# Four column groups for sums and gate logits, and one transposition for the one-hots of q and k, in a routed attention with a mixture of experts behind it

## The chip, the cores and the metric

The kernel runs on one core of a Trainium2 chip. The metric is the device time of one execution in microseconds (us). The core has a matrix engine (PE; its weight loads are listed apart as PEld), a vector engine (DVE), a scalar engine (ACT), a general engine (POOL) and DMA queues. Each engine works through its own instructions in order and waits for others by semaphores. All data is computed on in SBUF and PSUM, memories of 128 partitions.

## What is computed

Attention in which a query sees only those keys that fall to the same of 16 centroids, for 4 batches of 8 heads, 768 rows of 64 numbers; then a mixture of 8 experts that gives each row to one expert:

```python
q_assign = argmax(q_n @ c_n.T)            # per head; rows and centroids normalized
k_assign = argmax(k_n @ c_n.T)
mask = q_assign[:, :, :, None] == k_assign[:, :, None, :]
scores = where(mask, q @ k.T / sqrt(D), -1e9)
attn = exp(scores - max(scores)); attn = attn / (sum(attn) + 1e-9)
x = (attn @ v) -> rows of H*D             # 3072 x 512
logits = x @ w_gate; e = argmax(logits); gate = softmax(logits)[e]
out = gate * (relu(x @ w1[e]) @ w2[e])
```

## The kernel before

Attention goes over 16 pairs of heads (4 batches, 4 pairs each). A pair has 12 units: two halves of the queries (384 each) by six blocks of 128 keys. Three units make a turn, so a pair takes four turns. In one turn PE computes the scores of three units, does the jobs that the schedule puts there, multiplies the exponentials of the turn before with v, and does more jobs.

The mask is part of the score. Each row of q and k has a one-hot vector of its centroid. A second matmul adds q's one-hots times (one-hots of k - 1) * 2^60, so a score whose centroids differ becomes hugely negative before the exponential:

```python
def score(u):
    ...
    for a in range(2):          # the two heads: partitions 0-63 and 64-127
        r = slice(a * D, (a + 1) * D)
        nc.tensor.matmul(ps[:, a, 0:HS], lhsT=qk[g][r, 1, ks], rhs=qk[g][r, 0, qs], start=True, stop=False)   # L673
    for a in range(2):
        r = slice(a * D, (a + 1) * D)
        nc.tensor.matmul(ps[:, a, 0:HS], lhsT=ohT[g][r, 1, ks], rhs=ohT[g][r, 0, qs], start=False, stop=True) # L676
    A[u] = ap.tile([P, 2, HS], F32, name="A")
    nc.scalar.activation(A[u], ps[:, :, 0:HS], AF.Exp)                                                        # L678
    ...   # DVE adds A[u] to T, the running sum over key blocks                                              # L681, L685
```

The one-hots are made two turns ahead. `similar` (L613) multiplies q and k with the centroids, into four column groups of 32 PSUM partitions (q or k, by half); ACT copies the result, three transposes (L624) bring rows back to the partitions; `assign` and `assign2` find the largest and write the one-hots. One turn ahead `put` transposes them:

```python
ohs = consts.tile([P, 2 * NQ, 2, D], BF16, name="oh")     # 12 blocks: q and k apart, 2 heads x 64 columns, 16 used

def assign2(g):
    ...
    nc.vector.tensor_tensor(ohs[:, :, :, 0:C], rank..., top..., op=ALU.is_equal)                               # L641

def put(g):
    ohT[g] = ohp.tile([P, 2, S], BF16, name="ohT")
    ps = ps_s.tile([P, 2, 512], F32, name="sps").bitcast(BF16)
    for w in range(2):
        for j in range(NQ):
            nc.tensor.transpose(ps[:, w, j * P : (j + 1) * P], ohs[...], ident_b)                             # L651
    nc.scalar.copy(ohT[g][:, 0, :], ps[:, 0, 0:S])                                                            # L655
    nc.vector.tensor_scalar(ohT[g][:, 1, :], ps[:, 1, 0:S], scalar1=BIG, scalar2=-BIG, op0=ALU.mult, op1=ALU.add)  # L656
```

When a pair is done, its sums (over the 128 partitions of T) and its share of the gate logits are computed two turns later, the logits from the not yet divided rows XT. Before, a half of the queries has one column group of 32 PSUM partitions: 16 columns of logits for both heads, and the two sums:

```python
def weigh(g):
    ps = ps_m.tile([P, 512], F32, name="mps")
    t = [T.pop((g, half)) for half in range(2)]
    for i in range(3):
        for half in range(2):
            nc.tensor.matmul(
                ps[half * 32 : (half + 1) * 32, 0:HS],
                lhsT=one_row[:, i, :] if i < 2 else wg[:, g % HP, :],
                rhs=t[half][:, i, :] if i < 2 else XT[g][:, half * HS : (half + 1) * HS],
                start=(i == 0), stop=(i == 2))                                                                # L711
    lsT[g] = stat.tile([64, HS], F32, name="lsT", bufs=1)
    nc.scalar.copy(lsT[g], ps[0:64, 0:HS])                                                                    # L718

def weigh2(g):
    ...
    for i in range(NQ // 2):
        nc.tensor.transpose(ps[:, i * 64 : (i + 1) * 64], lt[:, i * P : (i + 1) * P], ident[0:64, 0:64])      # L725
    ls = stat.tile([P, NQ, 32], F32, name="ls")
    nc.vector.tensor_copy(ls, ps[:, 0 : NQ * 32]...)                                                          # L727
    ...   # reciprocal of the sums (L730), logits times it (L734), added to lg (L741, L744)
```

`x_turn` (L754, L757) transposes XT back and divides it, `gate` (L766 to L775) computes the softmax of a batch's logits, `turn` (L599 to L606) transposes the next q and k. Where they share a turn, the order in each engine is that of the program: the DVE operations of `weigh2`, then three additions to T, then, after a batch's last pair, `gate`, then L656 of `put`, then L757.

After attention the experts' matmuls follow (L301, L345); while the last pair's sums are computed, the first layer of an early group of rows runs in between.

Of the kernel before, what the change touches and what calls it, by code (L numbers as in the profile page):

```python
# [8 lines left out]
F32 = mybir.dt.float32  # L9
BF16 = mybir.dt.bfloat16  # L10
# [3 lines left out]
ALU = mybir.AluOpType  # L14
# [5 lines left out]
BIG = float(2**60)  # L20
# [163 lines left out]
def kernel(  # L184
# [11 lines left out]
    nc = tc.nc  # L196
    B, H, S, D = q.shape
    C = centroids.shape[1]
    P = 128
    NQ = S // P  # L200
    HP = H // 2
    NG = B * HP
    HS = S // 2
# [3 lines left out]
    E = moe_w_gate.shape[1]  # L207
    F = moe_w1.shape[2]
    DB = Dm // P
# [14 lines left out]
    consts = ctx.enter_context(tc.tile_pool(name="consts", bufs=1))  # L224
# [5 lines left out]
    def fetch(e, i):  # L230
        i %= 3
        w1 = wpools[i].tile([P, DB, F], F32, name=f"w1_{i}")
        w2 = wpools[i].tile([P, FB, Dm], F32, name=f"w2_{i}")
        nc.sync.dma_start(out=w1, in_=moe_w1[bass.ds(e, 1)].rearrange("e (a p) f -> p (e a) f", p=P))
        nc.sync.dma_start(out=w2, in_=moe_w2[bass.ds(e, 1)].rearrange("e (a p) d -> p (e a) d", p=P))
        return w1, w2
# [3 lines left out]
    ident = consts.tile([P, P], F32)  # L240
    ident_b = consts.tile([P, P], BF16)
# [18 lines left out]
    ps_s = late.enter_context(tc.tile_pool(name="ps_s", bufs=NB, space=PSUM))  # L260
# [4 lines left out]
    def wide():  # L265
        return ps_s.tile([P, 2, 512], F32, name="sps")
# [236 lines left out]
    with ExitStack() as actx:  # L503
        ld = actx.enter_context(tc.tile_pool(name="ld", bufs=2))
        qkp = actx.enter_context(tc.tile_pool(name="qkp", bufs=2))
        ohp = actx.enter_context(tc.tile_pool(name="ohp", bufs=2))
        asg = actx.enter_context(tc.tile_pool(name="asg", bufs=2))
        ap = actx.enter_context(tc.tile_pool(name="ap", bufs=2 * NB))
        tp_ = actx.enter_context(tc.tile_pool(name="tsum", bufs=2))
        stat = actx.enter_context(tc.tile_pool(name="stat", bufs=2))  # L510
# [27 lines left out]
        wg_in = consts.tile([P, DB, E], F32)  # L538
# [6 lines left out]
        first_c = iota("first_c", [P, C], [[-1, C]], C, 0)  # L545
        first_e = iota("first_e", [P, E], [[-1, E]], E, 0)

        wg = consts.tile([P, DB, 32], F32)
        nc.gpsimd.memset(wg, 0.0)
        one_row = consts.tile([P, 2, 32], F32)  # L550
        nc.gpsimd.memset(one_row, 0.0)
        for a in range(2):
            r = slice(a * D, (a + 1) * D)
            nc.gpsimd.tensor_copy(wg[r, :, a * E : (a + 1) * E], wg_in[r])
            nc.gpsimd.memset(one_row[:, a, 2 * E + a : 2 * E + a + 1], 1.0)

        ohs = consts.tile([P, 2 * NQ, 2, D], BF16, name="oh")
        nc.gpsimd.memset(ohs, 0.0)


        csq = consts.tile([P, D], F32)
# [27 lines left out]
        qk, sims, ohT = {}, {}, {}  # L589
# [47 lines left out]
        def assign2(g):  # L637
            rank = sims.pop(g)
            top = asg.tile([P, G], F32, name="top")
            nc.vector.tensor_reduce(top, rank, axis=AX, op=ALU.max)  # L640
            nc.vector.tensor_tensor(  # L641
                ohs[:, :, :, 0:C], rank.rearrange("p (t a) c -> p t a c", a=2),
                top.rearrange("p (t a) -> p t a", a=2).unsqueeze(3).to_broadcast([P, 2 * NQ, 2, C]), op=ALU.is_equal,
            )

        def put(g):
            ohT[g] = ohp.tile([P, 2, S], BF16, name="ohT")
            ps = ps_s.tile([P, 2, 512], F32, name="sps").bitcast(BF16)
            for w in range(2):
                for j in range(NQ):  # L650
                    nc.tensor.transpose(  # L651
                        ps[:, w, j * P : (j + 1) * P],
                        ohs[:, (j % (NQ // 2)) * 4 + w * 2 + j // (NQ // 2)].rearrange("p a c -> p (a c)"), ident_b,
                    )
            nc.scalar.copy(ohT[g][:, 0, :], ps[:, 0, 0:S])  # L655
            nc.vector.tensor_scalar(ohT[g][:, 1, :], ps[:, 1, 0:S], scalar1=BIG, scalar2=-BIG, op0=ALU.mult, op1=ALU.add)  # L656


        A, T, O = {}, {}, {}
        X, XT = {}, {}  # L660
# [43 lines left out]
        lsT, rds = {}, {}  # L704

        def weigh(g):
            ps = ps_m.tile([P, 512], F32, name="mps")
            t = [T.pop((g, half)) for half in range(2)]
            for i in range(3):
                for half in range(2):  # L710
                    nc.tensor.matmul(  # L711
                        ps[half * 32 : (half + 1) * 32, 0:HS],
                        lhsT=one_row[:, i, :] if i < 2 else wg[:, g % HP, :],
                        rhs=t[half][:, i, :] if i < 2 else XT[g][:, half * HS : (half + 1) * HS],
                        start=(i == 0), stop=(i == 2),
                    )
            lsT[g] = stat.tile([64, HS], F32, name="lsT", bufs=1)
            nc.scalar.copy(lsT[g], ps[0:64, 0:HS])  # L718

        def weigh2(g):  # L720
            b, hp = divmod(g, HP)
            lt = lsT.pop(g)
            ps = ps_m.tile([P, 512], F32, name="mps")
            for i in range(NQ // 2):
                nc.tensor.transpose(ps[:, i * 64 : (i + 1) * 64], lt[:, i * P : (i + 1) * P], ident[0:64, 0:64])  # L725
            ls = stat.tile([P, NQ, 32], F32, name="ls")
            nc.vector.tensor_copy(ls, ps[:, 0 : NQ * 32].rearrange("p (t r) -> p t r", r=32))  # L727
            den = ls[:, :, 2 * E : 2 * E + 2]
            rds[g] = stat.tile([P, NQ, 2], F32, name="rd")
            nc.vector.reciprocal(rds[g], den)  # L730
            nc.gpsimd.tensor_copy(dens[:, g, :].rearrange("p (t a) -> p t a", a=2), den)

            lgh = stat.tile([P, NQ, 2, E], F32, name="lgh")
            nc.vector.tensor_tensor(  # L734
                lgh, ls[:, :, 0 : 2 * E].rearrange("p t (a e) -> p t a e", a=2),
                rds[g].unsqueeze(3).to_broadcast([P, NQ, 2, E]), op=ALU.mult,
            )
            lgb = lg.rearrange("p (b h i) e -> p b i h e", b=B, h=2)[:, b]
            lgv = lgh.rearrange("p (i h) a e -> p i h a e", h=2)
            if hp == 0:  # L740
                nc.vector.tensor_tensor(lgb, lgv[:, :, :, 0, :], lgv[:, :, :, 1, :], op=ALU.add)  # L741
            else:
                for a in range(2):
                    nc.vector.tensor_tensor(lgb, lgb, lgv[:, :, :, a, :], op=ALU.add)  # L744
# [50 lines left out]
        for g in range(NG):  # L795
            n = g * TG
            if g == 1:

                for f, a in ((turn, (g, 0)), (turn, (g, 1)), (similar, (g,)), (similar2, (g,))):
                    at(-1 if f is similar2 else -2, 1, f, *a)  # L800
            else:
                at(n - 4, 0, turn, g, 0)
                at(n - 4, 1, turn, g, 1)
                at(n - 3, 0, similar, g)
                at(n - 3, 1, similar2, g)
            at(n - 2, 0, assign, g)
            at(n - 2, 0, assign2, g)
            at(n - 1, 0, put, g)
            at(n + TH, 1, finish, g, 0)
            at(n + 2 * TH, 1, finish, g, 1)  # L810
            if g < NG - 1:
                at(n + TG + 2, 0, weigh, g)
                at(n + TG + 2, 1, weigh2, g)
                at(n + TG + 3, 1, x_turn, g, 0)
                at(n + TG + 4, 0, x_turn, g, 1)
                if g % HP == HP - 1:
                    at(n + TG + 3, 0, gate, g // HP)
                    at(n + TG + 4, 0, keep_rows, g // HP)
# [51 lines left out]
        n = NG * TG  # L870
        at(n + 1, 0, first_half, 0, 0, FB // 4)
        at(n + 1, 0, weigh, NG - 1)
        at(n + 1, 0, first_half, 0, FB // 4, FB // 2)
        at(n + 1, 0, weigh2, NG - 1)
        at(n + 1, 0, x_turn, NG - 1, 0)
        at(n + 1, 1, x_turn, NG - 1, 1)
# [28 lines left out]
    with tc.tile_pool(name="sm", bufs=1) as sm:  # L905
# [31 lines left out]
        for t0 in range(0, NT, TQ):  # L937
# [11 lines left out]
            op=ALU.is_le,  # L949
# [3 lines left out]
        den = dens.rearrange("p g t -> p (g t)")  # L953
# [60 lines left out]
    with tc.If(nx > XU):  # L1014
        with tc.For_i(XU, nx, 1) as i:
# [4 lines left out]
            g = dict(n=[P], rows=N, w=fetch(ex, 0), gi=lambda j: gi[:, 0:1], si=lambda j: gi[:, 1:2], apart=False)  # L1020
# [36 lines left out]
```

## Time and profile before

| what | value |
| --- | --- |
| time, median of 3 executions | 864.28 us (863.96 to 864.37) |
| span of the profiled execution | 862.4 us |
| first 430 us (attention) | PE busy 396.3 of the 400 us from 30 to 430, DVE 244.2, ACT 207.2, POOL 27.5 |
| rest (430 to 862.4 us) | PE busy 417.4 of 432.4 us, DVE 52.7, ACT 50.2 |
| L711, sums and logits | 128 + 64 instructions on PE |
| L651, transposes of one-hots | 192 on PE |
| L725, transposes of sums and logits | 48 on PE |
| L656, one-hots of k to SBUF | 16 on DVE, 551 ns each |

How to read it: an fp32 matmul of the program is two instructions on PE in the trace, except the transposes. The ends of matmuls are modelled and overlap, so the cost of a stretch on PE is best taken from start to start. A line of the timeline merges neighbours of one kind: start, time from the first start to the last end, engine, line, operation, output and inputs, shapes, count, and in brackets how long the engine had been idle before and what ended it.

### The profile page before, as it was taken

To read this page: it belongs to the slowest core of one execution; us is meant where nothing else is said; L and a number is where in the kernel's file an instruction comes from. 1 tells how busy PE (TensorE), PEld (TensorE's weight loads), DVE (VectorE), ACT (ScalarE), POOL (GpSimd) and SP (SyncE) were. 2 spreads that over 40 slices of the span, in tenths; PEclk is the share of its full clock that TensorE was granted. 3 is DMA by queue.
4 is the path that set the end of the run, shared out by engine and by line. 5 is a ranking of instruction groups with operands and counts; after the bars stand their busy time and mean duration, and the time that the engine had idled before them with its cause. 6 is when DMAs were issued, how large, how long until landed. Compare 5 with 4: busy or idle time off the path is not lost.

```text
span 862.4 us, 10765 instructions
## 1 busy us (share of the span) xinstructions
PE 832.5 (97%) x4397; PEld 435.3 (50%) x4397; DVE 307.7 (36%) x543; ACT 271.2 (31%) x422; POOL 107.4 (12%) x165
## 2 busy tenths in 40 slices
PE   4999999999999999999999999999999999999994
PEld 3444544444445444444576646645444454545472
DVE  2655566565565665875543101010101010101000
ACT  3554544554545555544311111111111111110010
POOL 3000000000000000130004211302020303010010
PEclk8999999999999999999999999999999999999998
DMA  9025320482222122210060245434242423312010
GB/s 203 1 57 217 88 55 11 121 251 56 55 81 59 46 55 56 93 38 1 8 274 15 66 141 205 159 110 152 110 150 110 164 98 119 136 67 90 24 38 7
DMA packets 76186, 81.69 MB, mean 95 GB/s; under 512 B 52831, under 2 KB 56927, under 8 KB 75616
## 3 DMA queue, kind: packets, MB, share of 16 engines
q1 hardware_dynamic: 70208, 60.82, 23.0%
q0 software_dynamic: 5248, 20.04, 6.5%
q8 instruction: 37, 0.61, 0.3%
q14 instruction: 21, 0.17, 0.1%
q10 hardware_dynamic: 672, 0.05, 0.1%
HBM read 68.26 MB, written 13.68 MB: 95 GB/s over the span
## 4 chain that ended last, share of the span: by engine, by line
PE 46%; issue 38%; POOL 8%; DVE 5%; ACT 1%; DMA 0%; POOLq 0%; ACTq 0%; DVEq 0%
PE sps L673 14%; PE O L693 14%; PE mps L711 4%; PE sps L676 3%; POOL out_dram L316 3%; POOL xg L270 3%; PE sps L599 3%; PE sps L301 2%; PE mps L613 2%; DVE T L685 2%; PE sps L754 2%; PE sps L651 1%; POOL oh_c L468 1%; PE mps L624 1%; PE sps L345 1%
## 5 line engine op out<-in xcount | busy, mean ns | idle before, releaser
L678 ACT ACTIVATE A<-sps 128x768 f32<-128x768 f32 x192 | 154.4, 810 | 71.1 <-PE sps L676 70.0
L301 PE MATMUL sps<-xgT,w 128*128 128x416 f32 (+2 forms) x640 | 175.2, 434 | 1.1 <-ACT xgT L290 1.1
L673 PE MATMUL sps<-qk 64*128 64x384 f32 x768 | 163.7, 501 | 0.5 <-DVE x L757 0.5
L345 PE MATMUL sps<-w,h_sb 128*128 128x512 f32 x368 | 160.6, 595 | 1.3 <-DVE h_sb L309 0.9
L301 PEld LDWEIGHTS sps<-xgT,w 128*128 128x128 f32 x640 | 111.1, 190 | 67.5 <-issue 49.8
L685 DVE TENSOR_TENSOR T<-T,A 128x768 f32<-128x768 f32 x128 | 122.6, 958 | 47.6 <-ACT A L678 37.6
L693 PE MATMUL O<-A,v_in 128*64 128x384 f32 x768 | 138.0, 494 | 0.0
L309 DVE TENSOR_SCALAR h_sb<-sps 128x416 f32<-128x416 f32 (+2 forms) x34 | 18.7, 550 | 316.6 <-PE sps L301 316.6
L345 PEld LDWEIGHTS sps<-w,h_sb 128*128 128x128 f32 x368 | 69.1, 190 | 91.7 <-issue 85.6
L673 PEld LDWEIGHTS sps<-qk 64*128 64x128 f32 x768 | 68.1, 187 | 36.5 <-issue 33.7
L693 PEld LDWEIGHTS O<-A,v_in 128*64 128x64 f32 x768 | 49.4, 136 | 69.7 <-issue 68.2
L315 ACT ACTIVATE zo<-sps,xg 128x512 f32<-128x512 f32 (+1 forms) x34 | 23.3, 685 | 180.0 <-PE sps L345 171.0
L316 POOL DMA_INDIRECT out_dram<-zo,s_idx x34 | 33.0, 970 | 319.0 <-ACT zo L315 316.1
L676 PE MATMUL sps<-ohT 64*128 64x384 bf16 x384 | 66.2, 324 | 2.2 <-DVE ohT L656 2.2
L311 ACT ACTIVATE h_sb<-sps 128x416 f32<-128x416 f32 (+2 forms) x34 | 16.5, 484 | 162.8 <-DVE h_sb L309 162.8
L681 DVE SCALAR_TENSOR_TENSOR T<-A 128x768 f32<-128x768 f32 x32 | 30.7, 959 | 82.1 <-ACT A L678 82.1
L634 POOL TENSOR_TENSOR sim<-sim,first_c 128x384 f32<-128x384 f32 x16 | 16.0, 997 | 291.3 <-DVE sim L633 291.3
L270 POOL DMA_INDIRECT xg<-x_rows,g_idx x34 | 33.3, 980 | 22.8 <-issue 9.8
L676 PEld LDWEIGHTS <-ohT 64*128 64x128 bf16 x384 | 22.1, 94 | 26.5 <-DVE ohT L656 5.4
L701 ACT COPY xT<-O 128x384 f32<-128x384 f32 x32 | 15.4, 481 | 31.4 <-PE O L693 31.4
L711 PE MATMUL mps<-T,one_row 128*32 128x384 f32 x128 | 23.7, 492 | 0.0
L345 PE MATMUL sps<-w,h 128*128 128x512 f32 x48 | 21.3, 597 | 1.4 <-ACT h L311 1.4
(191 smaller groups left out, 532.2 us busy)
## 6 DMA issues: line engine op xcount, KB each, us to landing
w<-in_moe_w_dram SPq DMA_DIRECT2D x20, 2048.0 KB, 8.7
x_rows<-x POOLq DMA_DIRECT2D x4, 1548.0 KB, 7.2
q_in<-in_q_dram SPq DMA_DIRECT2D x32, 192.0 KB, 4.5
k_in<-in_k_dram SPq DMA_DIRECT2D x32, 192.0 KB, 4.6
v_in<-in_v_dram SPq DMA_DIRECT2D x16, 384.0 KB, 3.4
xg<-x_rows,g_idx POOLq DMA_INDIRECT x34, 5.1
out_dram<-zo,s_idx POOLq DMA_INDIRECT x34, 2.9
csb<-in_centroids_dram ACTq DMA_DIRECT2D x1, 32.0 KB, 1.8
```

The lines of the kernel that those rows point to most:

```text
L270: nc.gpsimd.indirect_dma_start(out=g["xg"][0:m, j, :], out_offset=None, in_=x_d[0 : g["rows"], :], in_offset=bass.IndirectOffsetOnAxis(ap= ...
L301: nc.tensor.matmul(o, lhsT=g["w"][0][:, c, fb * P : (fb + 1) * P], rhs=g["xT"][:, c, :cols], start=(c == 0), stop=(c == DB - 1),)
L316: ins = nc.gpsimd.indirect_dma_start(out=out[:, :], out_offset=bass.IndirectOffsetOnAxis(ap=g["si"](j)[0:m], axis=0), in_=zo[0:m], in_offs ...
L345: nc.tensor.matmul(zp, lhsT=g["h"][:, fb, j * P : (j + 1) * P], rhs=g["w"][1][:, fb, :], start=(fb == 0), stop=(fb == FB - 1),)
L599: nc.tensor.transpose(ps[:, i * P : (i + 1) * P], rows[g, "qk"[w]][:, j].rearrange("p a d -> p (a d)"), ident)
L673: nc.tensor.matmul(ps[:, a, 0:HS], lhsT=qk[g][r, 1, ks], rhs=qk[g][r, 0, qs], start=True, stop=False)
L676: nc.tensor.matmul(ps[:, a, 0:HS], lhsT=ohT[g][r, 1, ks], rhs=ohT[g][r, 0, qs], start=False, stop=True)
L678: nc.scalar.activation(A[u], ps[:, :, 0:HS], AF.Exp)
L681: nc.vector.scalar_tensor_tensor(T[g, half], in0=A[u - 1], scalar=1e-9 / P, in1=A[u], op0=ALU.add, op1=ALU.add)
L685: nc.vector.tensor_tensor(T[g, half], T[g, half], A[u], op=ALU.add)
L693: nc.tensor.matmul(O[g, half][a * D : (a + 1) * D, 0:HS], lhsT=rows[g, "v"][:, a, j, :], rhs=a_[:, a, :], start=(j == 0), stop=(j == NQ - 1),)
L711: nc.tensor.matmul(ps[half * 32 : (half + 1) * 32, 0:HS], lhsT=one_row[:, i, :] if i < 2 else wg[:, g % HP, :], rhs=t[half][:, i, :] if i ...
```

## The change

`weigh` uses all four column groups of 32 partitions, one per half and head, so each has to take only two matmuls, the sum and the logits of its own head, where a group took three before. Its result then fills 128 partitions, and the three transposes in `weigh2` are 128x128. In `put` the one-hots of q and k of a block of rows lie side by side (32 columns each, head by head) and are transposed together: six transposes and not twelve. A transposed block holds q's one-hots of a head at partitions 0 (or 64) and k's at 32 (or 96). ACT copies the whole block as the q side; for the k side, which must lie at the same partitions as q's, DVE reads k's 16 rows of each head and writes them shifted by 32 partitions into a tile whose other rows stay zero from the start. So what ACT copied of k is multiplied by zero. The two tiles for that are kept for the whole kernel and used in turn, as the pool's two buffers were before.

```diff
-        wg = consts.tile([P, DB, 32], F32)
+        wg = consts.tile([P, DB, 2, 32], F32)
-        one_row = consts.tile([P, 2, 32], F32)
+        one_row = consts.tile([P, 32], F32)
+        nc.gpsimd.memset(one_row[:, E : E + 1], 1.0)
...
-        ohs = consts.tile([P, 2 * NQ, 2, D], BF16, name="oh")
+        ohs = consts.tile([P, NQ, 2, 2, 32], BF16, name="oh")
         nc.gpsimd.memset(ohs, 0.0)
+        ohTs = []
+        for i in range(2):
+            t = consts.tile([P, 2, S], BF16, name=f"ohT{i}")
+            nc.gpsimd.memset(t[:, 1, :], 0.0)
+            ohTs.append(t)
...
         def assign2(g):
-            nc.vector.tensor_tensor(
-                ohs[:, :, :, 0:C], rank.rearrange("p (t a) c -> p t a c", a=2), ..., op=ALU.is_equal,
-            )
+            for w in range(2):
+                nc.vector.tensor_tensor(
+                    ohs.rearrange("p (i h) a w c -> p i (h a) w c", h=2)[:, :, :, w, 0:C], v(rank, w), ...,
+                    op=ALU.is_equal,
+                )
...
         def put(g):
-            ohT[g] = ohp.tile([P, 2, S], BF16, name="ohT")
-            ps = ps_s.tile([P, 2, 512], F32, name="sps").bitcast(BF16)
-            for w in range(2):
-                for j in range(NQ):
-                    nc.tensor.transpose(ps[:, w, j * P : (j + 1) * P], ohs[...], ident_b)
-            nc.scalar.copy(ohT[g][:, 0, :], ps[:, 0, 0:S])
-            nc.vector.tensor_scalar(ohT[g][:, 1, :], ps[:, 1, 0:S], scalar1=BIG, scalar2=-BIG, op0=ALU.mult, op1=ALU.add)
+            oh = ohT[g] = ohTs[g % 2]
+            ps = wide()[:, 0, :].bitcast(BF16)
+            for j in range(NQ):
+                nc.tensor.transpose(ps[:, j * P : (j + 1) * P], ohs[...], ident_b)
+            nc.scalar.copy(oh[:, 0, :], ps[:, 0:S])
+            for a in range(2):
+                nc.vector.tensor_scalar(
+                    oh[a * D : a * D + C, 1, :], ps[a * D + 32 : a * D + 32 + C, 0:S],
+                    scalar1=BIG, scalar2=-BIG, op0=ALU.mult, op1=ALU.add,
+                )
...
         def weigh(g):
-            for i in range(3):
+            for i in range(2):
                 for half in range(2):
-                    nc.tensor.matmul(ps[half * 32 : (half + 1) * 32, 0:HS], ...)
-            lsT[g] = stat.tile([64, HS], F32, name="lsT", bufs=1)
-            nc.scalar.copy(lsT[g], ps[0:64, 0:HS])
+                    for a in range(2):
+                        r = (2 * half + a) * 32
+                        nc.tensor.matmul(
+                            ps[r : r + 32, 0:HS], lhsT=wg[:, g % HP, a, :] if i else one_row,
+                            rhs=XT[g][:, half * HS : (half + 1) * HS] if i else t[half][:, a, :],
+                            start=(i == 0), stop=(i == 1),
+                        )
+            lsT[g] = stat.tile([P, HS], F32, name="lsT", bufs=1)
+            nc.scalar.copy(lsT[g], ps[:, 0:HS])
...
         def weigh2(g):
-                nc.tensor.transpose(ps[:, i * 64 : (i + 1) * 64], lt[:, i * P : (i + 1) * P], ident[0:64, 0:64])
-            ls = stat.tile([P, NQ, 32], F32, name="ls")
+                nc.tensor.transpose(ps[:, i * P : (i + 1) * P], lt[:, i * P : (i + 1) * P], ident)
+            ls = stat.tile([P, NQ, 2, E + 1], F32, name="ls")     # 9 of each 32 columns are copied
```

## The prediction

> **What bounds the kernel now.** I read the page's busy table and slices first, then the PE timeline over one pair of heads in the attention phase (a pair is four turns, 25.5 us), then the DVE timeline of the same stretch. All times in us.
>
> ```profile
> PE 832.5 (97%) x4397; PEld 435.3 (50%) x4397; DVE 307.7 (36%) x543; ACT 271.2 (31%) x422; POOL 107.4 (12%) x165
> PE   4999999999999999999999999999999999999994
> ```
>
> PE is full from the second slice on, so PE work taken away should shorten the run unless something else then holds PE. The PE timeline shows the three parts the change touches:
>
> ```profile
> 178.43 0.85 PE L613 MATMUL mps<-qk,cblk 128*32 128x384 f32 x8
> 179.21 2.16 PE L693 MATMUL O<-A,v_in 128*64 128x384 f32 x12
> 181.30 0.55 PE L624 MATMUL mps<-ident,simT 128*128 128x128 f32 x3
> ...
> 184.40 1.48 PE L711 MATMUL mps<-T,one_row 128*32 128x384 f32 x8
> 185.71 0.81 PE L711 MATMUL mps<-xT,wg 128*32 128x384 f32 x4
> 186.46 2.16 PE L693 MATMUL O<-A,v_in 128*64 128x384 f32 x12
> 188.54 0.33 PE L725 MATMUL mps<-ident,lsT 64*128 64x64 f32 x2
> ...
> 191.35 0.84 PE L651 MATMUL sps<-ident_b,oh 128*128 128x128 bf16 x12
> 192.12 2.16 PE L693 MATMUL O<-A,v_in 128*64 128x384 f32 x12
> 194.21 0.55 PE L754 MATMUL sps<-ident,xT 128*128 128x128 f32 x3
> 194.69 0.92 PE L673 MATMUL sps<-qk 64*128 64x384 f32 x4
> 195.44 0.33 PE L676 MATMUL sps<-ohT 64*128 64x384 bf16 x2
> ```
>
> Only the starts are used: a part costs the distance from its start to the next part's. L711 (`weigh`) takes 184.40 to 186.46, L651 (`put`) 191.35 to 192.12. The last line is the first use of the transposed one-hots of the pair, and here the other engine matters:
>
> ```profile
> 189.44 0.56 DVE L641 TENSOR_TENSOR oh<-sim,top 128x384 bf16<-128x384 f32 x1
> 189.92 0.35 DVE L727 COPY ls<-mps 128x192 f32<-128x192 f32 x1
> ...
> 191.23 3.08 DVE L685 TENSOR_TENSOR T<-T,A 128x768 f32<-128x768 f32 x3
> 194.23 0.55 DVE L656 TENSOR_SCALAR ohT<-sps 128x768 bf16<-128x768 bf16 x1
> 194.79 0.56 DVE L757 TENSOR_TENSOR x<-sps,rd 128x384 f32<-128x384 f32 x1
> ```
>
> From 188.85 to 195.35 DVE runs without a gap. L656 ends at 194.78 and PE uses its result at 195.44: a slack of 0.66, on an engine that is busy 36% of the span. Where the gating of a batch falls in between, the slack is gone already (L676 in the weight-load timeline):
>
> ```profile
> 144.37 0.10 PEld L676 LDWEIGHTS <-ohT 64*128 64x128 bf16 x2 [1.28 <-DVE ohT L656]
> ```
>
> **What the Trainium skill says.** "TensorEngine Tiling (Array Packing)", Tiling Modes: with 128 rows and 32 columns the array is four independent tiles. The trace agrees: L613, already in four column groups, starts its 8 fp32 instructions and is done in 0.78, while L711 in two groups needs 2.06 for 12. "VectorE: DVE Perf Modes", Why `tensor_reduce` can't reduce along partition axis: each of the 128 lanes is a pipeline of its own that streams the free dimension. So I expect an operation on 16 partitions to last as long as one on 128; before shows no narrow twin of L656, but L718 (64x384) takes 472 ns against 479 ns for L618 (128x384) on ACT. The same page, Two Vector instructions with no wait between them: an instruction whose input or output starts in another quadrant of 32 partitions than the last one's is held until every earlier one has finished. Before agrees: the two L578 operations (all 128 partitions) last 0.37 each and 0.47 together, the two L586 copies (partitions 0 and 64) 0.22 each and 0.46 together. Otherwise neighbours overlap: L656 at 143.76 lasts 0.56 and its successor starts at 144.23, 0.47 later.
>
> **The change part by part, for one ordinary pair.**
> PE:
> - `weigh`: 3 steps of two groups become 2 steps of four. A step is two instructions for each fp32 matmul, the column groups beside each other. L613 is an entry and one step, 0.78; L711 an entry and three steps, 2.06; so a step is 0.64 and the entry 0.14. New: 0.14 + 2 x 0.64 = 1.42. **-0.64**.
> - `put`: 12 transposes become 6: 0.77/2. **-0.38**.
> - `weigh2`: three transposes of 64 rows by 64 become 128 by 128. From 188.54 to that turn's first L676 at 189.41 is 0.87; the same stretch behind the three 128x128 fp32 transposes of L624 is 181.30 to 182.52, 1.22. The 64-row ones had been slipping in between the 64-row scores. **+0.35**.
> - Sum **-0.67**; scores and O are as before.
> DVE, in the chain that ends in the one-hots:
> - is_equal of 384 becomes two of 192. L641 to its successor is 0.48, of which 0.40 is 384 elements at the rate that 558 against 258 ns (L641 384 elements, L734 96) gives; a half is then about 0.28, two 0.56. **+0.08**.
> - `ls` copies 108 instead of 192 elements: at the same rate **-0.09**.
> - L656 becomes two operations of the same 768 elements, reading from partitions 32 and 96, writing to 0 and 64. Both are held: the first starts 0.08 later than by overlap, the second right behind its end (+0.02 as between the L586 pair) and lasts 0.55. **+0.65**.
> - Sum **+0.64** until PE has both halves.
> ACT copies as much as before (lsT 128 partitions, one half of ohT), POOL clears more at the start but ends about when PE needs it. No transfer changes.
>
> PE comes 0.67 earlier to L676, DVE delivers 0.64 later. The slack of 0.66 loses 0.07 for semaphore and weight load (144.32 end, 144.37 weights, matmul about 0.02 later), so 0.59 is usable. New wait: 0.67 + 0.64 - 0.59 = 0.72, net **+0.05 a pair**: the gain on PE is turned into a wait. It doesn't build up from pair to pair: two turns earlier DVE stood idle for 3.69 before L681, until ACT delivered, so the chain starts afresh from PE's scores in every pair. But PE's savings all lie between that start and L676, which is why the wait can swallow them.
>
> **All pairs.** The same slack (end of L656 to first L676) read at each of the 16:
> - 8 ordinary ones of 0.55 to 0.67: about +0.05 each, +0.4.
> - 2 wide ones, 0.96 and 0.90: -0.2 each, -0.4.
> - 3 behind a batch's gating and 1 behind the early routing (wait of 0.86 before the L676 weights at 377.33): PE waits there now; DVE's 0.64 is paid in full, +2.6.
> - pair 1, which has no sums before it: slack 0.20, and its `put` waits for the one-hots: 0.08 + 0.65 - 0.13, +0.6.
> - pair 0 at the start: transposes 1.46 become 0.73, DVE +0.57: -0.2.
> - the sums of the last pair but one have no one-hots behind them: -0.64 + 0.35 = -0.3. The last pair's lie in the PE-bound tail: -0.64, transposes about +0.05 (0.33 to 0.38 there): -0.6.
> Sum +2.1, 866.4. Against this: the halves come apart, so head 0's one-hot matmul (0.16) can be over before head 1's weights come, and up to 0.16 of each of 15 waits may be saved, 2.4. I take a third of it: **865.6**.
>
> **The rivals.**
> 1. PE's gain comes through: 0.67 x 14 + 0.38 + 0.3 + 0.6 = 10.7, about 853.5. For it speaks the 97% of PE. Against it the DVE chain without a gap. I give it one in ten in whole or in great part; it needs the new DVE pair to be much shorter than 2 x 0.55.
> 2. The two shifted operations overlap as aligned ones do: the chain grows by 0.08 - 0.09 + 0.47 = 0.46 instead of 0.64, and 15 times 0.18 less gives about 863. For it speaks that no wait stands between them in the program order of DVE; against it the L586 pair.
> 3. Four column groups with four different moving operands do not run at once. Then `weigh` gains nothing or loses 0.6 a pair, and the time goes to about 868 to 875. Against it L613, which has four different moving operands too.
> 4. The held operation delays x (L757) and through it the PSUM buffer of the third score unit: x would end near 196.0, the buffer is wanted at about 196.4. Not binding, by 0.4.
>
> **Range and chances.** Rivals 2 and the early half of the one-hot matmul pull down by 2 to 3, a longer shifted operation pulls up by 0.55 x its error x 15. I set 861 to 868.5. Even rival 1 in full (1.2%) stays within 2%, so nearly all weight is on the same.
>
> **What the new profile should show.** The L711 line's successor starting 1.42 behind it; the one-hot transposes 6 a pair in 0.38; the three lsT transposes lengthening the stretch to the first one-hot matmul to 1.2; two DVE operations of 16x768 at 0.55 each, 0.57 from start to start; PE busy time lower, and PE waiting on ohT in nearly every pair, about 0.7 in ordinary ones and near 2.6 behind a gate (1.28 + 0.67 + 0.64). If the waits on ohT stay few and the time falls by over 5, the chain argument is wrong; if `weigh` isn't 1.42, the tiling step is; if the two shifted operations are 0.47 apart, the held step is.

## The result, and the profile after

| | before | changed |
| --- | --- | --- |
| median | 864.12 us (863.90 to 864.37, 4 runs) | 868.25 us (866.77 to 868.92, 4 runs) |
| ratio | | 1.0045, 95% interval 1.0028 to 1.0063 |
| span of the profiled execution | 862.4 us | 866.2 us |

The changed kernel takes 0.45% longer, inside the predicted range (861 to 868.5) but 0.25 us from its upper end, and 2.7 us above the point predicted (865.6). PE has less to do and the span is longer. The page of the changed kernel, busy table and PE slices:

```profile
PE 828.6 (96%) x4365; PEld 427.7 (49%) x4365; DVE 318.1 (37%) x575; ACT 270.9 (31%) x422; POOL 108.4 (13%) x166
PE   4999999999999999999999999999999999999994
```

The PE timeline of the changed kernel, in the pair that the prediction was worked out on (`weigh` is now L726, its transposes L739, `put` L658, scores L685, one-hot matmuls L688, x L771):

```profile
183.60 0.33 PE L688 MATMUL sps<-ohT 64*128 64x384 bf16 x2
...
185.47 0.85 PE L726 MATMUL mps<-T,one_row 128*32 128x384 f32 x8
186.14 0.83 PE L726 MATMUL mps<-xT,wg 128*32 128x384 f32 x8
186.90 2.16 PE L705 MATMUL O<-A,v_in 128*64 128x384 f32 x12
188.99 0.55 PE L739 MATMUL mps<-ident,lsT 128*128 128x128 f32 x3
...
190.21 0.33 PE L688 MATMUL sps<-ohT 64*128 64x384 bf16 x2
...
192.09 0.51 PE L658 MATMUL sps<-ident_b,oh 128*128 128x128 bf16 x6
192.53 2.16 PE L705 MATMUL O<-A,v_in 128*64 128x384 f32 x12
...
196.00 0.33 PE L688 MATMUL sps<-ohT 64*128 64x384 bf16 x1
196.60 0.33 PE L688 MATMUL sps<-ohT 64*128 64x384 bf16 x1 [0.26 <-DVE ohT L665]
196.60 0.98 PE L685 MATMUL sps<-qk 64*128 64x384 f32 x4
197.35 0.39 PE L688 MATMUL sps<-ohT 64*128 64x384 bf16 x2
```

From start to start, the sums take 186.90 - 185.47 = 1.43 us and the one-hot transposes 0.44; from the lsT transposes to that turn's first one-hot matmul it is 190.21 - 188.99 = 1.22. So PE has its part of the saving. But the two heads' first one-hot matmuls of the next pair now start 0.60 apart, each behind DVE. DVE in the same stretch:

```profile
190.52 0.63 DVE L648 TENSOR_TENSOR oh<-sim,top 128x192 bf16<-128x192 f32 x2
191.07 0.27 DVE L742 COPY ls<-mps 128x108 f32<-128x108 f32 x1
...
192.29 3.08 DVE L697 TENSOR_TENSOR T<-T,A 128x768 f32<-128x768 f32 x3
195.40 1.14 DVE L665 TENSOR_SCALAR ohT<-sps 16x768 bf16<-16x768 bf16 x2
196.57 0.56 DVE L774 TENSOR_TENSOR x<-sps,rd 128x384 f32<-128x384 f32 x1
```

The two shifted operations (16 partitions, 0.55 each) start when the last addition has ended (192.29 + 3.08 = 195.37) and take 1.14, and x starts only behind them. In the weight-load timeline each head's one-hots now have a wait of their own, in every pair; it is longest behind a batch's gating:

```profile
248.55 0.09 PEld L688 LDWEIGHTS <-ohT 64*128 64x128 bf16 x1 [1.93 <-DVE ohT L665]
249.14 0.09 PEld L688 LDWEIGHTS <-ohT 64*128 64x128 bf16 x1 [0.50 <-DVE ohT L665]
```

A measure for all pairs: from the first one-hot matmul of the turn two ahead to that of the second unit of the pair, where the wait is over. In the pair above it is 197.35 - 183.60 = 13.75 us. Before, the two matmuls were these, 196.24 - 182.52 = 13.72 us apart:

```profile
182.52 0.33 PE L676 MATMUL sps<-ohT 64*128 64x384 bf16 x2
...
196.24 0.33 PE L676 MATMUL sps<-ohT 64*128 64x384 bf16 x2
```

PE's 0.67 are gone within this stretch. It is called "the stretch" below.

### The profile page after: what moved, and what is told of

It reads as the page before. It is cut to its first block, busy times and chain, and to the rows that moved or that the text cites. A ratio compares the mean times of both kernels' runs of the same rounds, so it can differ in the third digit from the quotient of the medians.

```text
span 866.2 us, 10734 instructions
## 1 busy us (share of the span) xinstructions
PE 828.6 (96%) x4365; PEld 427.7 (49%) x4365; DVE 318.1 (37%) x575; ACT 270.9 (31%) x422; POOL 108.4 (13%) x166
## 4 chain that ended last, share of the span: by engine, by line
issue 40%; PE 28%; DVE 18%; POOL 9%; ACT 3%; DMA 0%; POOLq 0%; DVEq 0%; ACTq 0%
PE sps L685 8%; PE O L705 8%; DVE T L697 7%; POOL out_dram L316 3%; POOL xg L270 3%; ACT A L690 3%; PE sps L603 3%; PE sps L688 3%; DVE ohT L665 2%; POOL sim L638 2%; PE sps L301 2%; DVE T L693 2%; PE mps L617 2%; DVE oh L648 1%; DVE sim L637 1%
## 5 line engine op out<-in xcount | busy, mean ns | idle before, releaser
L685 PE MATMUL sps<-qk 64*128 64x384 f32 x768 | 165.8, 505 | 0.6 <-DVE x L774 0.6
L697 DVE TENSOR_TENSOR T<-T,A 128x768 f32<-128x768 f32 x128 | 122.6, 957 | 49.0 <-ACT A L690 38.7
L685 PEld LDWEIGHTS sps<-qk 64*128 64x128 f32 x768 | 66.4, 187 | 37.2 <-issue 32.7
L688 PE MATMUL sps<-ohT 64*128 64x384 bf16 x384 | 71.2, 325 | 8.7 <-DVE ohT L665 8.5
L688 PEld LDWEIGHTS <-ohT 64*128 64x128 bf16 x384 | 22.9, 94 | 42.7 <-DVE ohT L665 22.0
L301 PE MATMUL sps<-xT,w 128*128 128x128 f32 x192 | 22.6, 277 | 0.0
```

The source lines that it names most:

```text
L301: nc.tensor.matmul(o, lhsT=g["w"][0][:, c, fb * P : (fb + 1) * P], rhs=g["xT"][:, c, :cols], start=(c == 0), stop=(c == DB - 1),)
L697: nc.vector.tensor_tensor(T[g, half], T[g, half], A[u], op=ALU.add)
```

## The experiments

Medians and ratios are against executions of the kernel before on the same chip. "Gate" is the softmax of a batch's logits, which falls behind three of the pairs (5, 9 and 13 of 0 to 15); pair 14 has the early routing in its way. "Ordinary" are pairs 3, 4, 7, 8, 11, 12 and 15; pairs 2, 6 and 10 depart from their figure in some rows (in the change +0.13, -0.21 and -0.21).

| kernel | median us | ratio to before, 95% | stretch against before, ordinary pair | gated pairs |
| --- | --- | --- | --- | --- |
| the change | 868.25 | 1.0045 (1.0028 to 1.0063) | +0.03 | +0.50 to +0.72 |
| sums alone | 859.42 | 0.9942 (0.9929 to 0.9955) | -0.33 | -0.09 |
| one-hots alone | 870.00 | 1.0074 (1.0060 to 1.0088) | +0.11 | +0.58 to +0.97 |
| before, L656 cut by head | 868.22 | 1.0044 (1.0032 to 1.0057) | 0.00 | +0.50 |
| before, L656 cut by columns | 865.25 | 1.0004 (0.9996 to 1.0012) | 0.00 | +0.06 |
| change, head 1 on ACT | 863.55 | 0.9986 (0.9979 to 0.9992) | -0.50 | +0.80 to +1.54 |
| change, gate later | 864.58 | 0.9998 (0.9990 to 1.0007) | +0.03 | -0.82 |
| before, gate later | 861.60 | 0.9966 (0.9954 to 0.9979) | 0.00 | -0.84 |
| sums alone, gate later | 856.50 | 0.9903 (0.9887 to 0.9918) | -0.33 | -1.18 |
| change, head 1 on ACT, gate later | 855.83 | 0.9901 (0.9885 to 0.9916) | -0.50 | -1.35 |
| change, both heads on ACT, gate later | 852.31 | 0.9858 (0.9843 to 0.9873) | -0.67 | -1.51 |

**Sums alone.** The new `weigh` and `weigh2` in the kernel before.

```diff
-            for i in range(3):            # two column groups
+            for i in range(2):            # four column groups, as in the change
```

> The sums and logits in four column groups alone; the one-hots as before. Theory A (PE's saving counts only where the vector engine's chain to the one-hots leaves room): PE -0.29 us a pair (-0.64 sums, +0.35 transposes), the chain 0.09 shorter, so no new wait; ten pairs at -0.29, the four that wait already at -0.09, the last two sums -0.9: about 860 us. Rival B (the four groups or the larger transposes give back what they save): 864 us or more, with the stretch of the sums above 1.6 us. Rival C (the four groups are worth their 0.64 in full, the larger transposes cost nothing): -0.64 x 16, about 854 us.

859.42 us, as theory A had it; B (864 or more) and C (854) fall. This half of the change is a gain of 0.6%: it takes 0.33 from PE in an ordinary pair, DVE's chain gets shorter and not longer, and the slack isn't used up.

**One-hots alone.** The new `assign2` and `put`, the old sums.

```diff
-            nc.vector.tensor_scalar(ohT[g][:, 1, :], ps[:, 1, 0:S], ...)
+            for a in range(2):
+                nc.vector.tensor_scalar(oh[a * D : a * D + C, 1, :], ps[a * D + 32 : a * D + 32 + C, 0:S], ...)
```

> The joint transposition of the one-hots alone; sums and logits as before. Theory A: PE -0.38 us a pair, the vector engine's chain +0.73 (two is_equal +0.08, two shifted operations +0.65), usable slack 0.59: +0.15 to +0.2 in ordinary pairs, -0.1 in the two wide ones, +0.73 where PE waits already: about 868 to 869 us; PE waits for ohT in nearly every pair. Rival B (the one-hot part is a gain on PE and the sums are what costs): -0.38 x 16, about 858 us. Rival D (the time above the sum of waits comes from the PE clock being halved for 3.4 us behind a long wait): 1.5 us more in a run in which the trace shows such a stretch.

870.0 us, 1 above theory A's 868 to 869: this half costs 0.7%, although PE has six transposes less in every pair. B is out. Six runs fell into four of 869.2 to 870.2 and two of 872.6 and 872.9, and the two have the lower mean clock of PE (0.988 against 0.993 to 0.995). That speaks for D, but these two have no trace that would show where the clock was halved.

**The cost on DVE alone.** The kernel before with its one operation cut by head, the same values computed and nothing taken from PE:

```diff
-            nc.vector.tensor_scalar(ohT[g][:, 1, :], ps[:, 1, 0:S], ...)
+            for a in range(2):
+                r = slice(a * D, (a + 1) * D)
+                nc.vector.tensor_scalar(ohT[g][r, 1, :], ps[r, 1, 0:S], ...)
```

> The kernel before, with its one operation on the one-hots of k cut in two by head (64 partitions each, no shift, same result): only the vector engine's cost of the change, nothing taken from PE. Theory A: the second starts when the first has ended and lasts 0.55, +0.57 us to the chain, which the slack of 0.59 takes up in ten pairs; the four waiting pairs +0.57 each, pair 1 +0.45, pair 0 +0.57: 864.1 + 3.3 to 3.8 = about 867.7 us. Rival F (the vector engine's extra time is paid in every pair): +0.57 x 16, about 873 us. Rival G (neighbours without a shift overlap, or half the partitions take half the time): within 0.5 us of before.

868.22 us, where theory A had about 867.7. The stretch is unchanged in the ordinary pairs to the hundredth, and 0.50 longer in the three gated ones, in the one with the early routing and in pair 1, which have no slack: F (paid everywhere) and G (paid nowhere) fall. DVE of this kernel, in an ordinary pair:

```profile
192.55 3.08 DVE L689 TENSOR_TENSOR T<-T,A 128x768 f32<-128x768 f32 x3
195.54 1.13 DVE L658 TENSOR_SCALAR ohT<-sps 64x768 bf16<-64x768 bf16 x2
196.71 0.56 DVE L761 TENSOR_TENSOR x<-sps,rd 128x384 f32<-128x384 f32 x1
```

Half the partitions take as long as all (0.55), and the second starts 0.57 to 0.58 behind the first. The first, which starts in partition 0 as the addition before it did, overlaps that addition (195.54 against its end at 195.63); the changed kernel's first operation, which starts in partition 32, doesn't. Is it the other partitions or just having two operations? Cut by columns:

```diff
+            for c in (slice(0, HS), slice(HS, S)):
+                nc.vector.tensor_scalar(ohT[g][:, 1, c], ps[:, 1, c], ...)
```

> The kernel before, with its operation on the one-hots of k cut in two by columns (384 each, all 128 partitions) and not by partitions. If what makes the second operation wait for the end of the first is the other start partition, these two overlap: about 0.27 from start to start, 0.07 us longer in all, and the time is within 0.5 us of before (864.3 to 864.8). If any two operations on this tile follow each other end to end, they start 0.35 to 0.38 apart, 0.16 to 0.2 longer in all, and the four waiting pairs, pair 0 and pair 1 make it about 865.3 us.

```profile
192.03 3.08 DVE L688 TENSOR_TENSOR T<-T,A 128x768 f32<-128x768 f32 x3
195.03 0.61 DVE L657 TENSOR_SCALAR ohT<-sps 128x384 bf16<-128x384 bf16 x2
195.59 0.56 DVE L760 TENSOR_TENSOR x<-sps,rd 128x384 f32<-128x384 f32 x1
```

Two operations of 0.35 in 0.61: 0.27 from start to start in all 16 pairs. Nor does it come from using only half of the partitions: the operation on x, on all 128, is held too behind the second head (196.71 behind its end at 196.67) and overlaps behind the cut by columns (195.59 against 195.64). So it is the other start partition that keeps the second from overlapping, as the Trainium skill has it ("VectorE: DVE Perf Modes", Two Vector instructions with no wait between them); two operations cut by columns cost next to nothing. The time is 865.25 us, 0.40 above the kernel before on the same chip (864.85): overlap was to stay within 0.5, the rival to add about 1.0. It is the trace that decides.

**One of the two operations taken off DVE.** Head 1's shift on ACT, behind its copy:

```diff
-            for a in range(2):
-                nc.vector.tensor_scalar(oh[a * D : a * D + C, 1, :], ps[a * D + 32 : a * D + 32 + C, 0:S], ...)
+            nc.scalar.activation(oh[D : D + C, 1, :], ps[D + 32 : D + 32 + C, 0:S], AF.Copy, scale=BIG, bias=-BIG)
+            nc.vector.tensor_scalar(oh[0:C, 1, :], ps[32 : 32 + C, 0:S], ...)
```

> The whole change, but the shifted operation of head 1 on the scalar engine, so that the vector engine has one and not two. Theory A: the chain is 0.07 longer than before instead of 0.65, ordinary pairs -0.52, wide ones -0.67, waiting ones +0.07 to +0.3: about 857 to 858 us. Rival E (the second operation on the vector engine is not what PE waits for; the wait comes from the first one, from the shared PSUM bank, or from the scalar engine's copy): stays at 866 to 869 us.

863.55 us, 6 above what was expected. The ordinary pairs did what theory A said (-0.50 to -0.52), so E falls; the gated ones lost 0.8 to 1.5 where 0.07 to 0.3 was expected (in pair 9, with the 1.5, PE ran at half clock from 245.26 on). ACT and DVE of this kernel there:

```profile
243.29 0.24 ACT L787 ACTIVATE ex<-ex 128x48 f32<-128x48 f32 x1 [2.74 <-DVE ex L784]
243.44 0.78 ACT L663 COPY ohT<-sps 128x768 bf16<-128x768 bf16 x1
...
244.24 0.80 ACT L664 ACTIVATE ohT<-sps 16x768 bf16<-16x768 bf16 x1
245.08 0.55 DVE L665 TENSOR_SCALAR ohT<-sps 16x768 bf16<-16x768 bf16 x1 [0.88 <-ACT ohT L664]
```

The gate's exponential stands ahead of `put` in ACT's order and waits for DVE; ACT's two operations on the one-hots come behind it, and DVE's own behind ACT's. Work moved to an idle engine had been put behind a wait on the engine it came from. So the next runs move the gate.

**Gate behind the one-hots**, first in the change:

```diff
-                    at(n + TG + 3, 0, gate, g // HP)
+                    at(n + TG + 3, 1, gate, g // HP)
```

> The whole change, with a batch's gating placed behind the one-hots of its turn and not ahead of them. Theory A: the three waits behind a gate become ordinary ones (stretch of 15.06 to 15.29 us down to 13.75), -1.3 each, and if the halved PE clock comes from those long waits, the 1.5 us of the profiled run of the change go too and no such stretch shows in the middle of the span: about 863 us (864 with, 862.5 without a share of the clock). Rival D' (the halved clock comes from something else than the long wait): the stretch at half clock stays somewhere in attention, about 864 to 865 us. Rival H (the gating only moves its time to another wait of PE): stays at 868.

864.58 us, 1.6 above what theory A gave. The gated pairs lose their extra wait (stretch -0.82 against before), and no stretch at half clock is left between the start and the end of the span, so D' falls by the trace, though the time lies in its range. H holds in part: behind the stretch pairs 5, 9 and 13 now take 0.41 longer than the others. ACT of pair 5 shows it:

```profile
145.85 0.24 ACT L788 ACTIVATE ex<-ex 128x48 f32<-128x48 f32 x1 [3.81 <-DVE ex L785]
146.00 2.19 ACT L690 ACTIVATE A<-sps 128x768 f32<-128x768 f32 x3
```

The gate's exponential now stands ahead of the exponentials of the scores. The first of these starts 1.07 behind the second head's one-hot matmul (144.93), where it was 0.37 in the pair shown above (196.97 behind 196.60); then PE's L603 waits for ACT. The same line in the kernel before:

> The kernel before with only the gating placed later, to have what that is worth without the change. Theory A: -0.84 us in three pairs (stretch of 14.56 down to 13.72): 864.3 - 2.5 = about 861.8 us. Rival H: no difference.

861.60 us, -0.84 in just these three pairs, and nothing of it comes back behind the stretch. With head 1 on ACT and the gate later:

> Head 1's shifted operation on the scalar engine and the gating later. Theory A: the scalar engine's operation is no longer caught behind the gating's exponential, all pairs gain what the ordinary ones did in the run before it (-0.5 to -0.67 each), the three gated ones 0.84 more: about 854 us, with no stretch at half clock in the middle. Rival E (the vector engine's second operation isn't the cause of the lost gain): not under 860 us.

855.83 us, 1.8 above what was expected; the ordinary pairs keep -0.50. Behind the stretch the three gated pairs take 0.54 longer each, 1.6 together, with A behind the gate's exponential again. With both shifts on ACT:

```diff
+            for a in range(2):
+                nc.scalar.activation(oh[a * D : a * D + C, 1, :], ps[a * D + 32 : a * D + 32 + C, 0:S], AF.Copy, scale=BIG, bias=-BIG)
```

> Both shifted operations on the scalar engine and the gating later: the vector engine has none left on the one-hots' chain. Theory A: PE's saving of 0.67 us comes through in full in every pair, if the scalar engine has copied and shifted (three operations of 0.8) before PE asks, which it should by about 0.3 us: about 852 us. If the scalar engine is late instead: PE waits for its ohT, about 854 to 857 us. Rival E: not under 860 us.

852.31 us, the best of all, 1.4% under before. PE and ACT of this kernel in the same pair (L687 is the one-hot matmul, L704 O):

```profile
187.31 0.51 PE L658 MATMUL sps<-ident_b,oh 128*128 128x128 bf16 x6
187.75 2.16 PE L704 MATMUL O<-A,v_in 128*64 128x384 f32 x12
189.84 0.55 PE L770 MATMUL sps<-ident,xT 128*128 128x128 f32 x3
190.31 0.92 PE L684 MATMUL sps<-qk 64*128 64x384 f32 x4
191.06 0.33 PE L687 MATMUL sps<-ohT 64*128 64x384 bf16 x2
```

```profile
188.13 0.79 ACT L663 COPY ohT<-sps 128x768 bf16<-128x768 bf16 x1
188.93 1.63 ACT L665 ACTIVATE ohT<-sps 16x768 bf16<-16x768 bf16 x2
```

ACT is ready at 190.56, PE asks at 191.06 and goes from score to one-hot matmul without a gap (0.75, as before). The stretch is 0.67 shorter in every ordinary pair: the saving that the change has on PE, in full. Last, to see what the joint transposition is worth once it isn't on DVE, the sums alone with the gate later:

> The sums in four column groups and the gating later, the one-hots as before: the version with the least changed, to set beside the one with both shifted operations on the scalar engine. Theory A: the gains add up, since neither fills the vector engine's slack: 859.4 - 2.8 - 3 x 0.25 = about 856 us, so the joint transposition on the scalar engine is worth the other 3.5 to 4 us. Rival I (the later gating alone would have given it all, or the gains overlap): 858 us or more.

856.50 us. So of the 12.4 us that the best version gains, the four column groups with the later gate give about 8.3 and the joint transposition, shifted on ACT, the other 4.

## Why the prediction was right, point by point

- *PE's part* (-0.64, -0.38, +0.35, sum -0.67): the sum shows as -0.67 where nothing takes it away again (both heads on ACT). Two of its terms are off and cancel, which is luck. The sums are 1.43 against 1.42. `put` is 0.44 against 0.38, -0.33 and not -0.38. The lsT transposes take 1.22 up to the first one-hot matmul, as worked out, but up to `put` 192.09 - 188.99 = 3.10, where it was 191.35 - 188.54 = 2.81: +0.29 and not +0.35.
- *DVE's part* (+0.64): +0.68 to +0.69 measured from the stretch's start to the end of the second operation. The mechanism of each term stood: halves of is_equal 0.28 apart, `ls` 0.27 instead of 0.35, the shifted pair held and 0.58 apart. The pair's term is mis-sized, about +0.70 instead of +0.65 from the end of the last addition. Rival 2 (overlapping, about 863) is out; that it is the start partition was shown by the two cuts of L656.
- *New wait, net +0.05 a pair*: the stretch is +0.03 in the ordinary pairs, and about 0.06 more goes behind it, since the second head's matmuls now trail the first one's by 0.06 up to the next part (198.16 to 198.48 is 0.32 where it was 0.26). +0.09 a pair in all, which is 0.68 less the usable slack of 0.59. Pair 10, counted as ordinary, has -0.15. Behind pair 9's gate the two weight loads wait 1.93 and 0.50, 2.4 together, where near 2.6 was named.
- *Waiting pairs* +2.6: +0.56, +0.56, +0.57 and +0.81, 2.5 together. In the last, pair 14, a score also waits for x, 0.6 where it was 0.5. *Pair 1* +0.6: +0.63. *Tail* -0.9: -1.0 from the last pair to the end. *Start* -0.2: -0.4, but the half clock at the start ended at 20.97 us in this execution and at 23.71 in the one before, so that is no measure of the change.
- *Wide pairs* -0.2 each: +0.19 in pair 2 and -0.15 in pair 6. The first is wrong: its DVE chain grew by 1.09. Of this 0.42 is an addition to T (L697), which starts 0.52 behind the end of the one before it (57.91 behind 57.39) instead of 0.10; what held it is not shown.
- *A third of 2.4 back because the heads come apart*: wrong, nothing came back (the trailing above is the opposite sign). Without it the sum was 866.4.
- *Missing from the sum*: 1.6 us of halved PE clock around pair 9, 0.2 within its stretch and 1.4 behind it (see the last section). The other terms come to +2.2 where the sum had +2.1, so the mechanism was right, the misses in single terms largely cancel, and the distance from 866.4 to 868.25 is nearly all the clock. That is read from the one execution with a trace; the prediction named no such cost, and its range only just covered it.
- Rival 1 is out by the stretches, rival 3 by the 1.43 of the sums, rival 4 in this pair by the third unit, whose scores start 0.16 behind the second's one-hot matmul (197.51 behind 197.35) in spite of the later x.

## What to carry to other kernels

A nearly full engine gains from work taken away only as far as its next operand is early: read the slack at the first use (0.66 us here) before counting the saving, and look for what the same change adds to the chain that delivers it. In these runs a DVE operation cut by partitions took twice its time (0.55 and 0.55), without overlap; cut it by columns where the work allows it, or give the second half to another engine. And when work goes to an engine with time left, see what stands ahead of it in that engine's order: here one small exponential that waits for another engine took back most of a good move. Placing it later helped, but in two of the five kernels with the later gate it held up the exponentials of the scores, which then stood behind it.

## What the runs showed of the hardware that was not expected

In two traces PE ran at half clock behind a long wait in attention. Busy time and granted clock of the changed kernel in four windows of 3.41 us around pair 9's wait (columns: window, its length, busy time and count of PE, PEld, DVE, ACT, POOL, then the PE clock, DMA share, GB/s):

```profile
242.84:246.26 3.42, 3.42 (x27) 1.42 (x21) 3.13 (x6) 1.39 (x2) 0.00 (x0) 1.00 0.00 0
246.26:249.67 3.41, 1.83 (x12) 0.85 (x12) 2.88 (x9) 1.03 (x3) 0.00 (x0) 1.00 0.00 0
249.67:253.08 3.41, 3.41 (x16) 1.93 (x12) 0.97 (x2) 2.14 (x3) 0.00 (x0) 0.50 0.00 0
253.08:256.50 3.42, 3.42 (x25) 1.94 (x23) 2.29 (x3) 0.86 (x3) 0.60 (x1) 1.00 0.14 60
```

Behind a window in which PE was busy 54% of the time, the clock is 0.50 for one window, and the same scores take twice as long (two one-hot matmuls of neighbouring units 1.60 apart instead of 0.81). From this pair's second unit to the start of the next pair's stretch the changed kernel takes 1.48 us longer than the one before; elsewhere that part is 0.06 longer. The Trainium skill, "TensorE: Matmul & The Clock Gate", What's actually happening, has windows of this length and the half rate, but names an idle window as the cause; here the window was half busy. With head 1 on ACT and the gate early a window with PE busy 50% did the same, while another in the changed kernel (from 352.07) with 54% didn't, so where the line lies stays open; the busy times rest on modelled ends. The busy share alone doesn't decide it: around the last matmuls, windows with 48% (kernel before, from 849.73) and 41% (changed, from 853.83) were followed by one at full clock. That the wait caused the halved clock fits these runs, but is not shown. In the change with the gate later no such window in attention behind the start was under 70% (attention ends near 430 us), no stretch at half clock appeared between the start and the end of the span, and the runs lay within 1.3 us of each other (863.9 to 865.1, 13 runs), where those with head 1 on ACT and the gate early lay between 860.6 and 864.7.
